# Smaller array tiles for the level and state matmuls of a gated linear attention, with a new order of issue

## The chip, the cores and the metric

The kernel runs on one core of one Trainium2 chip. The metric is the time on the device in microseconds (us), from the first to the last instruction; smaller is better. A profile is one execution taken by the hardware profiler.

## The reference

Two blocks follow each other. The first is a gated linear attention with complex decays: for every batch (4) and head (8), a 48 by 48 complex state is multiplied by a decay per row at each of 768 tokens, takes in the outer product of key and value, and is read by the query. The second is an MLP with a PReLU over all 3072 tokens.

```python
def _attn_ref(q, k, v, a_re, a_im):
    B, H, S, D = q.shape                      # 4, 8, 768, 48
    mag = np.sqrt(a_re * a_re + a_im * a_im)
    scale = np.minimum(mag, 0.999) / (mag + 1e-06)
    a_re_n, a_im_n = (a_re * scale, a_im * scale)
    ...
    for t in range(S):
        ar, ai = (a_re_n[:, :, t, :, None], a_im_n[:, :, t, :, None])
        new_re = ar * S_re - ai * S_im
        new_im = ar * S_im + ai * S_re
        kv = np.einsum('bhd,bhe->bhde', k[:, :, t], v[:, :, t])
        S_re, S_im = (new_re + kv, new_im)
        y[:, :, t] = np.einsum('bhd,bhde->bhe', q[:, :, t], S_re)
    return y

def _moe_ref(x, w_in, w_out, alpha):          # x: 3072 x 384, w_in: 384 x 2048, w_out: 2048 x 384
    h = x @ w_in
    g = np.maximum(h, 0.0) + alpha * np.minimum(h, 0.0)
    return (g @ w_out).astype(np.float32)
```

All matmuls are in fp32.

## The kernel before

The sequence is cut into chunks of 128 tokens; a **unit** is one chunk of one batch with all eight heads, so there are 24 units. The running products of the decays' phases and magnitudes come first (`gates`: VectorE, ScalarE, GpSimd; the results go through DRAM). In a unit, queries and keys are turned by the phases, so that real and imaginary parts stand as 96 rows (48 + 48). Inside a chunk, a pair of tokens (key s before query t) meets at exactly one **level** h of 1, 2, 4, 8, 16, 32: there the keys are those of the first half of a block of 2h tokens, the queries those of its second half. Each level thus has 64 keys and 64 queries for each head, and a mask keeps blocks of h by h on the diagonal. Between levels VectorE multiplies keys and queries by the decays over h tokens (`step`).

```python
    LEVELS = [1 << i for i in range(6)]
    ...
        def meet(name, weights, moving, n, *after):
            e = yield PE(0.467 * n / HC, ..., mode=1, n=8)
            t = ps.tile([P, HP, n], F32, tag="lv", name="ps_lv", bufs=2)     # HC = n = 64
            for p in range(4):
                for i in range(2):
                    nc.tensor.matmul(t[64 * i:64 * i + 64, p], lhsT=weights(4 * i + p),
                                     rhs=moving(KQ[:, 0, 4 * i + p]), start=True, stop=True)
        ...
        def mask_out(name, t, n, e):         # A[name] = ps_lv times the mask
            ...
            if name in by_row:               # h = 16 and 32: ScalarE, a mask by row
                for m, s in enumerate(by_row[name]):
                    cols = slice(m * name, (m + 1) * name)
                    nc.scalar.activation(a[:, :, cols], t[:, :, cols], AF.Copy, scale=s)
            else:                            # h = 1, 2, 4, 8: VectorE
                nc.vector.tensor_tensor(out=a, in0=t, in1=masks[name]..., op=ALU.mult)
```

A unit goes through six levels in turn: ScalarE copies the level's keys together (`W`, not for h = 1), TensorE lets them meet the queries (`ps_lv`), VectorE does the step, and the mask gives `A`.

```python
        for h in LEVELS:
            ...
                nc.scalar.copy(W..., halves(KQ[:, 1]..., h)[:, :, 0])
            e, t = yield from meet(h, weights, second(h), HC, w, k_)
            ...
            step(h)
            yield from mask_out(h, t, HC, e)
```

The two halves of a chunk then each give a **state product** (keys transposed, times values), one in the last chunk of a batch:

```python
        for n in range(H):                                          # 8 heads
            for s in range(1 if last else 2):                       # halves of 64 tokens
                rows = slice(HC * s, HC * (s + 1))
                nc.tensor.matmul(kv[s][:, n], lhsT=KT[rows, n],     # 64 rows, 96 weight columns
                                 rhs=V[rows, n // 2, (n % 2) * D:(n % 2 + 1) * D],
                                 start=True, stop=True)
```

The output `ps_y` sums the readout of the state (96 rows, 48 weight columns, 64 moving) and, for each level, values times `A` (64 by 48 weights, four tiles of the array). The MLP follows in groups of one or two chunks: `ps_h` (`w_in`), PReLU over ScalarE and VectorE (`g_sb`), `ps_o` (`w_out`).

The order in which all engines get their instructions is fixed while the program is built. A planner holds a model of engine times and, for each task (a gate group, a unit, the MLP, the loads), **due times** out of a table; at each point it issues, of the steps that can start within a small window, the one that is due first. A step on TensorE that would change the array's tiling is put back by `KEEP`.

```python
    KEEP = 569.0
    WINDOW = 0.185
    ...
            for task in self.tasks:
                t = self._start(task[1])
                ...
                    ready.append((first, not task[1][5], task[2][0] + self.KEEP * turn, len(ready), t, task))
            now = min(ready)[0] + self.WINDOW
            *_, t, task = min((r for r in ready if r[0] <= now), key=lambda r: r[1:4])
```

Of the kernel before, what the change touches and what calls it, by code (L numbers as in the profile page):

```python
# [9 lines left out]
F32 = mybir.dt.float32  # L10
U32 = mybir.dt.uint32
U16 = mybir.dt.uint16
AF = mybir.ActivationFunctionType
ALU = mybir.AluOpType
# [3 lines left out]
P = 128  # L18
# [26 lines left out]
class Plan:  # L45
# [6 lines left out]
    POOL = 0.4  # L52
# [3 lines left out]
    RATE = 215.0  # L56
    SWITCH = 0.095
    ENTER = (0.105, 0.048, 0.04, 0.053)
    KEEP = 569.0
    WINDOW = 0.185  # L60
    FETCH = 6.0
    COUNT = 84.0
    WAITS = 1.0107
# [71 lines left out]
                self.tasks.remove(task)  # L135


DUES = {'gates0': (-11979.6, -10892.9),
 'gates1': (174.7, -496.9),
 'gates2': (561.6, -311.9),  # L140
 'gates3': (3235.0, -200.5),
 'gates4': (1592.2, -63.0),
 'gates5': (4379.1, 219.4),
 'gates6': (489.8, 859.5),
 'gates7': (3140.3, 976.6),
 'gates8': (2306.3, 2393.8),
 'loads': (-377.6, 1731.8),
 'halves': (1898.2, -2044.1),
 'v': (-322.2, 1835.9),
 'raw': (2301.7, -5010.3),  # L150
 'in': (-1647.0, -796.9),
 'out': (3534.9, -230.2),
 'unit0': (-3641.5, -1502.8),
 'unit1': (-5353.3, -123.3),
 'unit2': (-1532.8, 1640.0),
 'unit3': (-36.9, 1543.1),
 'unit4': (-67.5, -25.0),
 'unit5': (-141.1, -113.0),
 'unit6': (1465.8, 2568.1),
 'unit7': (107.5, 119.9),  # L160
 'unit8': (181.8, 180.8),
 'unit9': (137.3, 195.5),
 'unit10': (387.8, 400.1),
 'unit11': (311.3, 312.9),
 'unit12': (681.4, 692.8),
 'unit13': (575.5, 570.7),
 'unit14': (910.0, 926.1),
 'unit15': (803.1, 798.4),
 'unit16': (1248.6, 1307.1),
 'unit17': (859.2, 964.8),  # L170
 'unit18': (1896.0, 2100.5),
 'unit19': (738.1, 831.9),
 'unit20': (913.8, 963.5),
 'unit21': (2733.6, 4210.5),
 'unit22': (-2826.2, 536.2),
 'unit23': (-402.2, 5283.7),
 'mlp': (-1586.9, 86.2)}

UNIT_STEPS = [-1.986, -14.344, -6.726, -1.525, -2.462, -10.149, -2.522, -4.692, -4.149, -10.103, -10.542, -0.315, -7.97,
 -6.489, -0.934, -9.318, -9.689, -5.484, -17.877, -60.052, -33.755, -3.423, -13.049, -34.345, -29.097, -2.452,  # L180
 -0.718, -31.551, 3.33, 0.026, 3.304, 6.38, -3.93, -14.011, -21.191, -7.962, -28.438, -0.376, -6.583, -1.248,
 -21.404, -25.972, -17.097, -22.461, 20.771, 1.493, -15.349, 0.052, 4.97, -13.972, 11.878, -14.379, 32.13,
 -21.617, 23.086, 22.986, 21.226, -2.184]


@with_exitstack
def kernel(
# [32 lines left out]
    nc = tc.nc  # L220
    B, HP, _, D, S = q.shape
# [5 lines left out]
    D2 = 2 * D  # L227
    HC = P // 2
# [13 lines left out]
    ps = ctx.enter_context(tc.tile_pool(name="ps", bufs=1, space=PSUM))  # L242

    def halves(t, h):

        return t.rearrange("p (n s h) -> p n s h", s=2, h=h)
# [4 lines left out]
    masks, by_row = {}, {}  # L251
# [16 lines left out]
    for h in (16, 32):  # L268
        by_row[h] = []
        for m in range(HC // h):  # L270
            t = consts.tile([P, 1], F32, tag=f"rows{h}_{m}", name=f"rows{h}_{m}")
# [6 lines left out]
    done = plan.done  # L278
# [5 lines left out]
        return "ACT", 0.17 + n * 0.85e-3, after, takes, 0, first  # L284

    def POOL(n, *after):
        return "POOL", 0.4 + n * 2.0e-3, after, (), 0, False

    def PE(us, *after, takes=(), mode=0, n=1):
        return "PE", us * plan.pace, after, takes, 0, False, mode, 4 * n  # L290

    def DMA(kb, *after, takes=(), engine="SP"):
        return engine, 0.45, after, takes, kb, False

    R = {name: Ring(n) for name, n in dict(
        KQ=3, PP=1, T=2, V=1, W=2, KT=1, St=3, yT=1, xT=2, raw0=1, raw1=1, raw2=1, g0=0, g1=0, g2=0, ot=2, top=2,
        lv=2, misc=1, y=1, h=2, o=1).items()}
# [250 lines left out]
    start = consts.tile([D2, B, H], F32, tag="start")  # L548
# [68 lines left out]
    def weights(name):  # L617
        for f in range(NF // 2):
            dst = w_in_sb[:, f] if name == "in" else w_out_sb[:, 2 * f:2 * (f + 1)]
            done["w_" + name, 2 * f] = done["w_" + name, 2 * f + 1] = yield from piece(dst, name, f)  # L620
# [102 lines left out]
    state = {}  # L723
# [5 lines left out]
    def unit(u):  # L729
# [3 lines left out]
        KQ, PP = L["KQ"], L["PP"]  # L733
# [2 lines left out]
        R["PP"].put(r)  # L736
        A, made = {}, []

        def meet(name, weights, moving, n, *after):

            e = yield PE(0.467 * n / HC, *after, *[("met", name, u - 1)] * (u > 0), takes=(R["lv"], R[name]), mode=1, n=8)
            t = ps.tile([P, HP, n], F32, tag="lv", name="ps_lv", bufs=2)
            for p in range(4):
                for i in range(2):
                    nc.tensor.matmul(t[64 * i:64 * i + 64, p], lhsT=weights(4 * i + p),  # L745
                                     rhs=moving(KQ[:, 0, 4 * i + p]), start=True, stop=True)
            done["met", name, u] = e
            return e, t

        def mask_out(name, t, n, e):  # L750

            if name in by_row:
                e = yield ACT(HP * name + 100, e)
            else:
                e = yield DVE(HP * n, e)
            a = A[name] = work.tile([P, HP, n], F32, tag=f"A{name}", name=f"A{name}",
                                    bufs=2 if name <= 4 else 1)
            if name in by_row:
                for m, s in enumerate(by_row[name]):
                    if m:  # L760
                        e = yield ACT(HP * name + 100, e)
                    cols = slice(m * name, (m + 1) * name)
                    nc.scalar.activation(a[:, :, cols], t[:, :, cols], AF.Copy, scale=s)  # L763
            else:
                a, t = [z.rearrange("p n (s t) -> p (n s) t", t=HC) for z in (a, t)]
                nc.vector.tensor_tensor(out=a, in0=t, in1=masks[name].unsqueeze(1).to_broadcast(
                    [P, HP * n // HC, HC]), op=ALU.mult)
            R["lv"].put(e)
            made.append(e)

        def second(h):
            return lambda t: halves(t, h)[:, :, 1]

        def step(h):

# [9 lines left out]
        if c == 0:  # L785
            k_ = yield DMA(144, *[("state", u - 2)] * (u > 1), takes=(R["St"],))
# [3 lines left out]
            k_ = yield DVE(H * D, k_, ("start", 0))  # L790
            nc.vector.tensor_tensor(out=St, in0=St, in1=start[:, b].unsqueeze(2).to_broadcast([D2, H, D]), op=ALU.mult)
            state[b] = (St, k_)
        k_ = r
        for h in LEVELS:
            w = k_
            if h == 1:
                weights = lambda n: KQ[:, 1, n].rearrange("p (m s) -> p m s", s=2)[:, :, 0]
            else:
                w = yield ACT(H * HC, k_, takes=(R["W"],))
                W = work.tile([D2, H, HC], F32, tag="W", name="W", bufs=2)  # L800
                nc.scalar.copy(W.rearrange("p n t -> p (n t)").rearrange("p (m h) -> p m h", h=h),  # L801
                               halves(KQ[:, 1].rearrange("p n t -> p (n t)"), h)[:, :, 0])
                weights = lambda n: W[:, n]
            e, t = yield from meet(h, weights, second(h), HC, w, k_)
            if h > 1:
                R["W"].put(e)
            k_ = yield DVE(2 * H * HC, e, *[("decays", u)] * (h == 1))
            T = L["T"]
            step(h)
            yield from mask_out(h, t, HC, e)  # L810
        q_ = k_

        last = c + 1 == NCH
        for i in range(2):
            e = yield PE(0.333, k_, takes=(R["misc"],), n=4)
            t = ps.tile([P, HP, D2], F32, tag="misc", name="ps_kt")
            for p in range(4):
                nc.tensor.transpose(t[:, p], KQ[:, 1, 4 * i + p], ident[:D2, :D2])  # L818
            e = yield ACT(HP * D2, e, takes=() if i else (R["KT"],))
            if i == 0:  # L820
                KT = work.tile([P, H, D2], F32, tag="KT", name="KT", bufs=1)
            nc.scalar.copy(KT[:, 4 * i:4 * i + 4], t)
            R["misc"].put(e)
        e = yield PE(1.395, e, ("V", u), *[("state", u - 1)] * (u > 0), takes=(R["misc"],) if last else (R["misc"], R["lv"]), mode=3, n=8 if last else 16)
        V = L["V"]
        kv = [ps.tile([D2, H, D], F32, tag=tag, name="ps_kv", bufs=n) for tag, n in (("misc", 1), ("lv", 2))[:2 - last]]
        for n in range(H):
            for s in range(1 if last else 2):
                rows = slice(HC * s, HC * (s + 1))
                nc.tensor.matmul(kv[s][:, n], lhsT=KT[rows, n], rhs=V[rows, n // 2, (n % 2) * D:(n % 2 + 1) * D],  # L830
                                 start=True, stop=True)
        R["KT"].put(e)
        states = [state.pop(b)]
        for s in range(1 if last else 2):
# [14 lines left out]
        g, cg = group_of[u]  # L849
        for s in range(2):  # L850
            before, known = states[s]
            e = yield PE(0.444, q_, known, takes=() if s else (R["y"],), mode=1, n=8)
            if s == 0:
                Y = ps.tile([P, 2, 512], F32, tag="y", name="ps_y")[:, :, 0:2 * P].rearrange(
                    "p i (s t) -> p i s t", s=2)
            for n in range(H):
                nc.tensor.matmul(Y[64 * (n % 2):64 * (n % 2) + D, n // 4, n // 2 % 2, HC * s:HC * (s + 1)],  # L857
                                 lhsT=before[:, n], rhs=KQ[:, 0, n, HC * s:HC * (s + 1)],
                                 start=(s == 0 and n // 2 % 2 == 0), stop=False)
            R["St"].put(e)  # L860
# [168 lines left out]
```

## Time and profile before

| what | value |
|---|---|
| time, median of three (lowest to highest) | 925.12 us (920.33 to 927.54) |
| TensorE busy, matmuls / weight loads | 756.7 us (82%) / 569.1 us (62%) |
| VectorE busy | 664.6 us (72%) |
| ScalarE busy | 412.2 us (45%) |
| GpSimd busy | 198.4 us (21%) |
| TensorE matmuls and weight loads recorded | 8384 each |
| DMA | 130.51 MB, 141 GB/s |

In the profile's lines, PE is TensorE's matmuls, PEld its weight loads, DVE VectorE, ACT ScalarE and POOL GpSimd. `L745` is line 745 of the kernel: L745 the levels, L830 the state products, L857 the state readout, L870 values times `A`, L917 `ps_h`, L936 `ps_o`, L783 the steps, L801 the copies `W`, L766 and L763 the masks. `96*64 96x64` after a matmul is its weights (rows by columns) and its moving operand (rows by columns). An fp32 matmul call shows as two records. The end of a matmul is modelled, so that busy times overlap; starts are measured. `issue` is time in which an engine waited for nothing that the profile shows; `q8 instruction` is the DMA queue that brings TensorE's instructions.

### The profile page before, as it was taken

The numbers are of one execution on the slowest core, as the hardware profiler recorded it, in microseconds if no ns is written. First come the engines' busy times: TensorE is split into PE (matmuls) and PEld (weight loads), VectorE is DVE, ScalarE is ACT, GpSimd is POOL, SyncE is SP. The second block draws the span as 40 slices with busy tenths as digits, with TensorE's granted clock in tenths as the row PEclk, the third lists the DMA queues.
The fourth block names the chain that finished last, engine by engine and source line by source line (L and its number), as shares of the span: only waits on it lengthen the run. The fifth ranks groups of instructions, "written<-read, shape, count | busy, mean of one in ns | idle before, by whom it ended". The sixth has DMA issues, their size and how long they took to land.

```text
span 923.7 us, 20680 instructions
## 1 busy us (share of the span) xinstructions
PE 756.7 (82%) x8384; PEld 569.1 (62%) x8384; DVE 664.6 (72%) x956; ACT 412.2 (45%) x897; POOL 198.4 (21%) x347
## 2 busy tenths in 40 slices
PE   0013423497998899999988999999999999999998
PEld 0002422375776677767766777777777777777776
DVE  5897988898997789979876977978674555531112
ACT  6554455364554456454754236543433333432111
POOL 4054183005400630280063015000700000000000
PEclk9999999999999999999998999999999999999999
DMA  8691985968778576958775586857565656420000
GB/s 223 147 270 52 222 217 163 242 155 166 141 191 193 120 161 150 208 101 190 194 142 108 164 185 124 181 117 169 115 138 109 131 121 112 104 61 18 18 9 18
DMA packets 194533, 130.51 MB, mean 141 GB/s; under 512 B 74504, under 2 KB 186248, under 8 KB 194440
## 3 DMA queue, kind: packets, MB, share of 16 engines
q1 hardware_dynamic: 194440, 129.20, 61.5%
q8 instruction: 66, 1.08, 0.5%
q14 instruction: 27, 0.22, 0.1%
HBM read 100.82 MB, written 35.71 MB: 148 GB/s over the span
## 4 chain that ended last, share of the span: by engine, by line
PE 67%; DVE 13%; POOL 9%; ACT 4%; issue 4%; DMA 1%; SPq 1%; DVEq 0%; ACTq 0%; POOLq 0%
PE ps_o L936 26%; PE ps_h L917 24%; PE ps_lv L745 7%; POOL gate L428 4%; POOL gate L430 4%; PE ps_y L870 3%; PE ps_kv L830 3%; PE ps_y L857 2%; DVE gate L428 2%; DVE KQ L783 2%; DVE gate L430 1%; PE ps_kt L818 1%; DVE gate L514 1%; POOL run L430 1%; DVE top L599 1%
## 5 line engine op out<-in xcount | busy, mean ns | idle before, releaser
L936 PE MATMUL ps_o<-w_out_sb,g_sb 128*128 128x384 f32 x768 | 301.7, 509 | 28.2 <-DVE g_sb L926 28.1
L917 PE MATMUL ps_h<-xT,w_in_sb 128*128 128x256 f32 (+1 forms) x1344 | 296.8, 356 | 3.3 <-issue 3.2
L917 PEld LDWEIGHTS ps_h<-xT,w_in_sb 128*128 128x128 f32 x1344 | 236.4, 193 | 76.5 <-issue 6.5
L926 DVE SCALAR_TENSOR_TENSOR g_sb<-g_sb,al,ps_h 128x256 f32<-128x256 f32 (+1 forms) x224 | 98.2, 439 | 170.4 <-ACT g_sb L924 169.1
L783 DVE TENSOR_TENSOR KQ<-KQ,T 96x1024 f32<-96x1024 f32 x144 | 176.2, 1234 | 32.8 <-PE ps_lv L745 29.4
L924 ACT ACTIVATE g_sb<-ps_h 128x256 f32<-128x256 f32 (+1 forms) x224 | 78.9, 353 | 257.7 <-PE ps_h L917 251.8
L936 PEld LDWEIGHTS ps_o<-w_out_sb,g_sb 128*128 128x128 f32 x768 | 132.9, 192 | 82.1 <-DVE g_sb L926 29.5
L745 PE MATMUL ps_lv<-KQ,W 96*64 96x64 f32 x1920 | 85.6, 239 | 70.5 <-ACT W L801 67.5
L745 PEld LDWEIGHTS ps_lv<-KQ,W 96*64 96x64 f32 x1920 | 70.7, 148 | 97.0 <-ACT W L801 76.3
L801 ACT COPY W<-KQ 96x512 f32<-96x512 f32 x120 | 74.6, 624 | 60.4 <-DVE KQ L783 59.0
L428 POOL TENSOR_TENSOR gate<-gate 128x72 f32<-128x72 f32 (+1 forms) x56 | 37.8, 674 | 146.9 <-ACT gate L458 143.2
L734 DVE TENSOR_TENSOR KQ<-KQ,PP 96x2048 f32<-96x2048 f32 x24 | 55.6, 2316 | 17.1 <-DMA PP<-phs 16.9
L745 PE MATMUL ps_lv<-KQ 96*64 96x64 f32 x384 | 17.8, 237 | 51.8 <-DVE KQ L734 50.0
L745 PEld LDWEIGHTS ps_lv<-KQ 96*64 96x64 f32 x384 | 14.8, 149 | 55.0 <-DVE KQ L734 50.2
L883 ACT COPY yT<-ps_y 48x256 f32<-48x256 f32 x96 | 30.9, 366 | 36.5 <-PE ps_y L870 33.9
L428 DVE TENSOR_TENSOR gate<-gate 128x576 f32<-128x576 f32 (+3 forms) x70 | 44.7, 639 | 1.7
L870 PE MATMUL ps_y<-A,VL 64*48 64x64 f32 x2304 | 42.7, 227 | 1.2 <-issue 1.2
L514 DVE TENSOR_TENSOR gate<-gate 128x1152 f32<-128x1152 f32 (+2 forms) x36 | 43.0, 1216 | 0.7 <-POOL gate L499 0.6
L830 PEld LDWEIGHTS ps_kv<-V,KT 64*96 64x96 f32 x704 | 37.0, 172 | 10.2 <-issue 6.8
L763 ACT ACTIVATE A<-ps_lv,rows 128x64 f32<-128x64 f32 x144 | 37.3, 331 | 12.6 <-PE ps_lv L745 12.2
L870 PEld LDWEIGHTS ps_y<-A,VL 64*48 64x48 f32 x2304 | 37.7, 126 | 8.0 <-issue 6.4
L430 POOL TENSOR_TENSOR gate<-gate 128x36 f32<-128x36 f32 (+1 forms) x56 | 40.5, 723 | 4.4
(94 smaller groups left out, 769.3 us busy)
## 6 DMA issues: line engine op xcount, KB each, us to landing
T<-decs SPq DMA_DIRECT2D x48, 384.0 KB
PP<-phs SPq DMA_DIRECT2D x48, 193.5 KB
KQ<-in_q_dram SPq DMA_DIRECT2D x48, 192.0 KB
decs<-gate SPq DMA_DIRECT2D x7, 1152.0 KB
phs<-gate SPq DMA_DIRECT2D x14, 576.0 KB
KQ<-in_k_dram SPq DMA_DIRECT2D x40, 192.0 KB
vsc<-in_v_dram SPq DMA_DIRECT2D x48, 144.0 KB
VL<-vsc SPq DMA_DIRECT2D x24, 288.0 KB
```

Source lines behind the costliest of these rows:

```text
L428: on(4 * k).tensor_tensor(out=m, in0=w[:, 1::-1].unsqueeze(2).to_broadcast([P, 2, 2, k]), in1=pairs_of(u), op=ALU.mult)
L430: on(2 * k).tensor_tensor(out=dst, in0=m[:, 0], in1=m[:, 1], op=ALU.add)
L734: nc.vector.tensor_tensor(out=KQ, in0=KQ, in1=bass.AP(tensor=PP.tensor, offset=PP.offset, ap=[PP.ap[0], (1, 2), (P + 1, H), (1, P)]), op=A ...
L745: nc.tensor.matmul(t[64 * i:64 * i + 64, p], lhsT=weights(4 * i + p), rhs=moving(KQ[:, 0, 4 * i + p]), start=True, stop=True)
L783: nc.vector.tensor_tensor(out=x, in0=x, in1=m, op=ALU.mult)
L801: nc.scalar.copy(W.rearrange("p n t -> p (n t)").rearrange("p (m h) -> p m h", h=h), halves(KQ[:, 1].rearrange("p n t -> p (n t)"), h)[:, ...
L830: nc.tensor.matmul(kv[s][:, n], lhsT=KT[rows, n], rhs=V[rows, n // 2, (n % 2) * D:(n % 2 + 1) * D], start=True, stop=True)
L870: nc.tensor.matmul(o, lhsT=Vp[h][64 * i:64 * i + 64, s, e_ * D:(e_ + 1) * D], rhs=a, start=False, stop=(h == LEVELS[-1] and s == 1))
L917: nc.tensor.matmul(p, lhsT=w_in_sb[:, f // 2, kk, f % 2 * P:(f % 2 + 1) * P], rhs=x_of[m][:, kk], start=(kk == 0), stop=(kk == NK - 1))
L924: nc.scalar.activation(gt, p, AF.Relu, scale=-1.0)
L926: nc.vector.scalar_tensor_tensor(out=gt, in0=gt, scalar=al_1[:, f:f + 1], in1=p, op0=ALU.mult, op1=ALU.add)
L936: nc.tensor.matmul(sums[0], lhsT=gt[:, c * P:(c + 1) * P], rhs=w_out_sb[:, f], start=(f == 0), stop=(f == NF - 1))
```

## The change

The matmuls of a level are cut to the blocks on the diagonal that the mask can keep: with h of at most 32, the first 32 keys only meet the first 32 queries, the second 32 the second. A level becomes 16 calls of 32 weight columns by 32 moving columns in place of 8 of 64 by 64, and writes four groups of 32 partitions, four column tiles of the array. `ps_lv` is half as wide; the mask's instructions read it twice. The state products are cut into three pieces of 32 weight columns: 48 calls in place of 16, on three column tiles by two row tiles. Both are meant to use more of the array at once. The planner's model is fitted anew (levels 0.28 in place of 0.467, state products 0.75 in place of 1.395), and with it the due times of all tasks, `KEEP` and `WINDOW`.

```diff
-    KEEP = 569.0
-    WINDOW = 0.185
+    KEEP = 180.0
+    WINDOW = 0.077
...
-DUES = {'gates0': (-11979.6, -10892.9),
- 'gates1': (174.7, -496.9),
...
- 'mlp': (-1586.9, 86.2)}
+DUES = {'gates0': (-5527.1, -5917.4),
+ 'gates1': (-86.9, -80.3),
...
+ 'mlp': (-3039.5, 582.0)}
...  (UNIT_STEPS, 58 numbers, replaced as well)
     def POOL(n, *after):
-        return "POOL", 0.4 + n * 2.0e-3, after, (), 0, False
+        return "POOL", 0.5 + n * 2.0e-3, after, (), 0, False
...
-            e = yield PE(0.467 * n / HC, ..., mode=1, n=8)
-            t = ps.tile([P, HP, n], F32, tag="lv", name="ps_lv", bufs=2)
+            e = yield PE(0.28, ..., mode=1, n=16)
+            t = ps.tile([P, HP, HC // 2], F32, tag="lv", name="ps_lv", bufs=2)
             for p in range(4):
                 for i in range(2):
-                    nc.tensor.matmul(t[64 * i:64 * i + 64, p], lhsT=weights(4 * i + p),
-                                     rhs=moving(KQ[:, 0, 4 * i + p]), start=True, stop=True)
+                    q_ = halves(KQ[:, 0, 4 * i + p], h)[:, :, 1]
+                    for g in range(2):
+                        j, m = HC // 2 * g, HC // (2 * h)
+                        nc.tensor.matmul(t[64 * i + j:64 * i + j + HC // 2, p], lhsT=weights(4 * i + p)[:, j:j + HC // 2],
+                                         rhs=q_[:, m * g:m * (g + 1)], start=True, stop=True)
...
-                    nc.scalar.activation(a[:, :, cols], t[:, :, cols], AF.Copy, scale=s)
+                    at = m * name % (HC // 2)
+                    nc.scalar.activation(a[:, :, cols], t[:, :, at:at + name], AF.Copy, scale=s)
             else:
-                a, t = [z.rearrange("p n (s t) -> p (n s) t", t=HC) for z in (a, t)]
-                nc.vector.tensor_tensor(out=a, in0=t, in1=masks[name].unsqueeze(1).to_broadcast(
-                    [P, HP * n // HC, HC]), op=ALU.mult)
+                whole = [P, HP, 2, HC // 2]
+                nc.vector.tensor_tensor(out=a.rearrange("p n (g t) -> p n g t", g=2), in0=t.unsqueeze(2).to_broadcast(whole),
+                                        in1=masks[name].rearrange("p (g t) -> p g t", g=2).unsqueeze(1).to_broadcast(whole),
+                                        op=ALU.mult)
...
-        e = yield PE(1.395, e, ("V", u), ..., mode=3, n=8 if last else 16)
+        e = yield PE(0.75, e, ("V", u), ..., mode=3, n=24 if last else 48)
...
-            for s in range(1 if last else 2):
-                rows = slice(HC * s, HC * (s + 1))
-                nc.tensor.matmul(kv[s][:, n], lhsT=KT[rows, n], rhs=V[rows, n // 2, (n % 2) * D:(n % 2 + 1) * D],
-                                 start=True, stop=True)
+            for j in range(0, D2, HC // 2):
+                for s in range(1 if last else 2):
+                    rows = slice(HC * s, HC * (s + 1))
+                    nc.tensor.matmul(kv[s][j:j + HC // 2, n], lhsT=KT[rows, n, j:j + HC // 2],
+                                     rhs=V[rows, n // 2, (n % 2) * D:(n % 2 + 1) * D], start=True, stop=True)
...
-            e = yield PE(0.444, q_, known, ..., mode=1, n=8)
+            e = yield PE(0.47, q_, known, ..., mode=1, n=8)
```

## The prediction

> **What bounds the kernel now.** I read the page's forty slices first, then the windows view (busy time by stage), then TensorE's waits, and last the timeline.
>
> ```profile
> PE   0013423497998899999988999999999999999998
> DVE  5897988898997789979876977978674555531112
> q8 instruction: 66, 1.08, 0.5%
> ```
>
> A slice is 23.1 us. TensorE has little to do in the first eight slices (185 us), while VectorE is busy; from there on it is full to the end. The windows view gives the same with numbers (columns: window, length, then busy us and instructions of PE, PEld, DVE, ACT, POOL, clock, DMA):
>
> ```profile
> 0.00:185.00 185.00, 45.55 (x652) 38.15 (x652) 153.03 (x243) 96.74 (x158) 63.01 (x106) 1.00 0.76 192
> 185.00:300.00 115.00, 104.22 (x1355) 81.57 (x1354) 100.63 (x149) 61.40 (x141) 24.29 (x44) 0.96 0.76 170
> 300.00:500.00 200.00, 188.00 (x2078) 138.66 (x2077) 166.84 (x214) 104.96 (x223) 74.16 (x116) 0.97 0.72 158
> 500.00:700.00 200.00, 198.83 (x2176) 147.46 (x2176) 157.41 (x209) 85.51 (x205) 36.88 (x80) 1.00 0.65 144
> ```
>
> So there are two stages. The head, 0 to 185 us, is bound by the gates' chain over VectorE, ScalarE and GpSimd; TensorE is idle for 139 of its 185 us. In the rest, 739 us, TensorE sets the end. Its waits, over the whole span, say the same (us in total, times, longest):
>
> ```profile
> PE ps_lv L745 <- ACT W L801: 67.5, 20, 15.5
> PE ps_lv L745 <- DVE KQ L734: 50.0, 2, 47.9
> PE ps_o L936 <- DVE g_sb L926: 28.1, 3, 25.0
> PE ps_lv L745 <- issue: 4.4, 3, 1.8
> PE ps_h L917 <- issue: 3.2, 1, 3.2
> ```
>
> The same view cut to the head holds 56.0, 50.0 and 25.0 us of the first three. After 500 us TensorE waits once in all, 1.2 us. **A microsecond of TensorE's time saved after 185 us is therefore worth about a microsecond at the end; one saved before it is worth next to nothing.**
>
> What a level and a state product occupy is read from starts, not from the modelled busy time. Timeline of TensorE (start, us, instructions merged):
>
> ```profile
> 501.92 1.46 PE L917 MATMUL ps_h<-xT,w_in_sb 128*128 128x256 f32 x6
> 503.31 1.15 PE L745 MATMUL ps_lv<-KQ,W 96*64 96x64 f32 x32
> 504.39 1.56 PE L936 MATMUL ps_o<-w_out_sb,g_sb 128*128 128x384 f32 x4
> ...
> 511.77 1.56 PE L830 MATMUL ps_kv<-V,KT 64*96 64x48 f32 x32
> 513.26 1.56 PE L917 MATMUL ps_h<-xT,w_in_sb 128*128 128x256 f32 x6
> ...
> 529.49 0.69 PE L745 MATMUL ps_lv<-KQ,W 96*64 96x64 f32 x16
> 530.11 1.56 PE L936 MATMUL ps_o<-w_out_sb,g_sb 128*128 128x384 f32 x4
> ```
>
> An fp32 call is two records, so one level (8 calls) is x16. From a start to the next line's start, two levels take 1.08 us and one 0.62: a level costs **0.46 us**, and leaving this tiling costs 0.62 - 0.46 = 0.16. Entering costs about 0.10 more (six ps_h records take 1.39 us ahead of ps_lv, 1.29 ahead of a full-array line at 505.79 to 507.08). A state product, x32, takes 1.49 - 0.15 for leaving = **1.34 us**, a little more in blocks entered from cold.
>
> **What the Trainium skill says.** "TensorEngine Tiling (Array Packing)", Key Properties: tiles run weight loads and matmuls in parallel, and a change of tiling drains the engine. The trace agrees on both: single records of ps_lv start in pairs, 7 ns apart in the pair and 58 ns from pair to pair (two column tiles side by side), and entering plus leaving costs the 0.26 us above. The same page, Instruction Overhead: about 60 cycles a matmul, and no tiling factor should be taken from a dimension that is already small. That would speak against 32 columns; but the ps_y line (64x64 tiles, four at once) starts records 7 ns apart, so the overhead isn't serial across tiles here. "TensorE: Matmul & The Clock Gate", LDWEIGHTS: a load's time goes with its columns. It fits the state product: two row tiles with 96 weight columns take 85 ns a pair for only 48 moving columns, whereas ps_y with 48 weight columns moves 64 columns on four tiles in 56 ns. The same page, Part 3, gives 2.38 times for three column tiles and 10.6 for sixteen tiles; no run here has shown 32-column tiles yet.
>
> **The change part by part.**
>
> *Levels.* A level's 64 keys by 64 queries need only the two diagonal 32x32 blocks (the mask drops the rest for block sizes to 32), so 8 calls become 16 with half the weight columns and half the moving columns, on four column tiles. Now: 8 rounds of two tiles at 58 ns = 0.46 us. After: 32 records in 8 rounds of four. A round is bound by its moving columns, half of 58 = 29 ns, or by starts, 4 x 7 = 28 ns. That makes 8 x 29 = 0.23 us; the diff's own planner figure is 0.28. I take 0.26 between them, so 0.20 saved. The windows view cut to L745 counts 992 + 1040 = 2032 records after 185 us, which is 127 of the 144 levels: 127 x 0.20 = **25.4 us**. The 17 levels of the head shorten a chain that waits for other engines: under 3 us, left out.
>
> *State products.* 16 calls become 48 with 32 weight columns, on three column groups by two row groups. Now 1.34. After: 96 records in 16 rounds of six; starts 6 x 7 = 42 ns, moving columns 48/64 x 56 = 42 ns: 0.67 us; the planner's figure is 0.75. I take 0.71, so 0.63 saved. Cut to L830 the windows view has 288 + 352 = 640 records after 185 us: 18 blocks of 32 and the four shorter ones of a batch's last chunk (16). 18 x 0.63 + 4 x 0.31 = **12.6 us**.
>
> *Mask-out.* VectorE still writes 128x256 elements (413 ns now, L766), reading the smaller ps_lv twice by a broadcast; ScalarE's instructions are the same in number and size. Nothing. The state readout (L857) is untouched; the planner's 0.47 in place of 0.444 is 1 us over all units, left out.
>
> *More instructions.* TensorE's 8384 + 8384 records grow by 144 x 32 for levels and 1408 x 2 for states, to 24,192. The instruction queue brings them in 66 packets of 1.08 MB, some 256 instructions each, so 29 more packets are needed, bunched in the new blocks. Issue waits of TensorE after 185 us are 3.2 + 1.8 + 1.2 = 6.2 us now. With 44% more instructions and denser bunches I take **5 us lost**.
>
> *Due times.* They alter nothing but order. From 185 us on the trace shows 169 visits to a tiling (94 levels, 22 states, 23 readouts, 30 outputs), at 0.26 us each 44 us in all: not less than what the change saves. The planner's penalty for a switch falls from 569 to 180 and its look-ahead from 0.185 to 0.077, which lets it switch more readily; I take 12 visits more, **3 us lost**, by choice rather than by reading.
>
> Sum: 25.4 + 12.6 - 5 - 3 = 30 us. 925 - 30 = **895 us**.
>
> **Rivals.** (1) *The 32-column tiles don't run four at once*: loads or starts become serial, a level stays near 0.42 us and a state near 1.1. Then 127 x 0.04 + 20 x 0.24 = 10 us are saved and 8 given back: about 923. Against it stands ps_y, whose four tiles hold 14 ns a record. (2) *VectorE becomes the bound.* From 185 to 700 us it is busy for 100.6 + 166.8 + 157.4 = 425 of 515 us, 82%; with 25 us of that stage gone it is 87%. A third of the gain could turn into waits of levels for VectorE, about 905; against it, MLP matmuls stand ready to fill, and 84 us of them are left over at the end. (3) *The new order is the larger part.* If the head gets filled with more TensorE work or switches become fewer, 875 to 880; if the new times stretch the head (139 us idle there, a 47.9 us first wait) or let fetches and switches bunch, 925 to 945.
>
> **Range and chances.** The tile arithmetic alone gives 38 saved, give or take 8; fetch and switches 8 lost, give or take 6; order in the head give or take 12. Together some 16 either way, more for rival 1: 873 to 918. The 2% line is at 906.6. Faster by over 2%: 0.75; within 2%: 0.17; slower by over 2%: 0.08.
>
> **What would show it.** Right: ps_lv reads 96*32 with x32 a level, 0.23 to 0.28 us from first start to last; ps_kv shows 64*32 with x96 in 0.67 to 0.75 us; the head is still about 185 us; TensorE stays at nine tenths from there to the end; q8 has about 95 packets. Wrong: a level stays over 0.4 us (rival 1); after 300 us ps_lv waits for W or KQ by tens of us (rival 2); issue waits over 15 us (fetch mis-sized); visits off by over 30, or the first full slice of TensorE a slice or more from where it is now (rival 3).

## The result and the profile after

The changed kernel takes 897.69 us (median of four, 891.59 to 900.16) against 922.73 us for the kernel before beside it: a ratio of 0.9716, 95% interval 0.9643 to 0.979. The prediction said 895. The sum came out; the two terms that make it up did not, and most of this part is about that.

The slices of the page, with the granted clock of TensorE and the queue that brings its instructions:

```profile
PE   0000143877979899999989999998999999999998
DVE  5997989998969898879878988895677555532112
PEclk9999995788989999999999999999999999999999
q8 instruction: 95, 1.56, 0.8%
```

95 packets are what the prediction worked out. TensorE stands at eight tenths in slice 8 already, where it stood at four before, so the head ends about a slice earlier. New are dips (7, 8) in TensorE's row after the head and half or reduced clock in slices 7 to 10 and 12. The windows view, columns as before:

```profile
0.00:185.00 185.00, 44.84 (x1140) 36.28 (x1140) 161.62 (x256) 103.09 (x175) 59.05 (x106) 0.92 0.80 200
185.00:300.00 115.00, 99.42 (x1925) 74.32 (x1926) 99.77 (x145) 57.77 (x128) 32.62 (x55) 0.90 0.70 163
300.00:500.00 200.00, 190.44 (x3365) 136.53 (x3365) 170.93 (x221) 108.45 (x236) 62.09 (x106) 0.98 0.73 163
500.00:700.00 200.00, 195.09 (x3268) 140.18 (x3268) 154.81 (x208) 88.62 (x210) 42.73 (x80) 0.98 0.70 153
```

Between 185 and 300 us TensorE is busy for less (99.4 in place of 104.2 us) and the clock is 0.90 in place of 0.96; from 500 to 700 us, where it was full, 195.1 in place of 198.8. So some of the time that the smaller tiles free is idle. TensorE's waits after the head (185 us on; us in total, times, longest):

```profile
PE ps_lv L748 <- issue: 7.0, 3, 3.3
PE ps_kt L822 <- ACT KT L826: 6.2, 2, 3.9
PE ps_h L922 <- DMA xT<-ysc: 4.0, 2, 2.5
PE ps_lv L748 <- ACT W L805: 4.0, 4, 2.7
PE ps_y L875 <- issue: 2.3, 2, 2.0
PE ps_o L941 <- issue: 1.8, 2, 1.6
```

Issue waits are 13.9 us in all (two kinds of 1.5 and 1.3 us are not shown), against 6.2 before. The blocks themselves, in the timeline:

```profile
500.46 0.46 PE L748 MATMUL ps_lv<-KQ,W 96*32 96x32 f32 x32
500.85 1.56 PE L941 MATMUL ps_o<-w_out_sb,g_sb 128*128 128x384 f32 x4
...
521.93 1.09 PE L835 MATMUL ps_kv<-V,KT 64*32 64x48 f32 x96
522.95 1.56 PE L941 MATMUL ps_o<-w_out_sb,g_sb 128*128 128x384 f32 x4
```

A level, with leaving, takes 0.39 us; leaving has become shorter (0.125 us by single records), so the level is 0.27. A state product takes 1.02 with leaving, so 0.89: less than the 1.34 of before, more than the 0.71 that I took.

### The profile page after: what moved, and what is told of

It reads as the page before. It is cut to its first block, busy times and chain, and to the rows that moved or that the text cites. A ratio compares the mean times of both kernels' runs of the same rounds, so it can differ in the third digit from the quotient of the medians.

```text
span 897.6 us, 28109 instructions
## 1 busy us (share of the span) xinstructions
PE 721.5 (80%) x12096; PEld 526.4 (59%) x12096; DVE 662.6 (74%) x956; ACT 412.8 (46%) x897; POOL 196.6 (22%) x347
## 4 chain that ended last, share of the span: by engine, by line
PE 52%; DVE 15%; DMA 10%; POOL 7%; SPq 7%; ACT 5%; issue 4%; DVEq 0%; ACTq 0%; POOLq 0%
PE ps_o L941 21%; PE ps_h L922 19%; SPq L714 4%; POOL gate L428 4%; PE ps_y L875 3%; PE ps_lv L748 3%; DMA PP<-phs 3%; DMA T<-decs 2%; POOL gate L430 2%; DVE gate L428 2%; PE ps_y L862 2%; PE ps_kv L835 2%; DVE KQ L787 2%; DVE gate L430 2%; DVE KQ L734 1%
## 5 line engine op out<-in xcount | busy, mean ns | idle before, releaser
L922 PE MATMUL ps_h<-xT,w_in_sb 128*128 128x256 f32 (+1 forms) x1344 | 300.8, 358 | 4.2 <-DMA xT<-ysc 4.0
L748 PE MATMUL ps_lv<-KQ,W 96*32 96x32 f32 x3840 | 56.3, 204 | 82.0 <-ACT W L805 70.9
L748 PEld LDWEIGHTS ps_lv<-KQ,W 96*32 96x32 f32 x3840 | 44.5, 116 | 110.7 <-ACT W L805 83.4
L428 POOL TENSOR_TENSOR gate<-gate 128x72 f32<-128x72 f32 (+1 forms) x56 | 40.6, 725 | 172.5 <-ACT gate L458 168.8
L748 PE MATMUL ps_lv<-KQ 96*32 96x32 f32 x768 | 12.0, 204 | 58.5 <-DVE KQ L734 57.1
L875 PE MATMUL ps_y<-A,VL 64*48 64x64 f32 x2304 | 44.7, 227 | 2.3 <-issue 2.3
L748 PEld LDWEIGHTS ps_lv<-KQ 96*32 96x32 f32 x768 | 9.5, 117 | 62.3 <-DVE KQ L734 57.3
L772 DVE TENSOR_TENSOR A<-ps_lv,mask 128x256 f32<-128x256 f32 x96 | 39.3, 413 | 0.0
```

What stands on the lines that cost most here:

```text
L428: on(4 * k).tensor_tensor(out=m, in0=w[:, 1::-1].unsqueeze(2).to_broadcast([P, 2, 2, k]), in1=pairs_of(u), op=ALU.mult)
L748: nc.tensor.matmul(t[64 * i + j:64 * i + j + HC // 2, p], lhsT=weights(4 * i + p)[:, j:j + HC // 2], rhs=q_[:, m * g:m * (g + 1)], start=T ...
L875: nc.tensor.matmul(o, lhsT=Vp[h][64 * i:64 * i + 64, s, e_ * D:(e_ + 1) * D], rhs=a, start=False, stop=(h == LEVELS[-1] and s == 1))
L922: nc.tensor.matmul(p, lhsT=w_in_sb[:, f // 2, kk, f % 2 * P:(f % 2 + 1) * P], rhs=x_of[m][:, kk], start=(kk == 0), stop=(kk == NK - 1))
```

## Experiments

In what follows, `work`, `waits` and `half clock` are worked out from the starts of all matmul records after 185 us. Each gap between two starts is compared with the mean gap of the same pair of shapes at full clock; an excess over 0.4 us counts as a wait, a smaller excess inside a stretch of half clock as half clock (time lost, not the length of the stretch), the rest is work. The three, and some 4 us at the very end, make up the span after the head.

### Tiles and order apart

Four kernels. Two keep one order and change the tiles: the planner's figures and due times stay, and with them the order of all instructions on all engines. Old tiles in the new order:

```diff
 # the changed kernel's planner figures and due times
-  16 calls of 32 x 32 for a level, 48 of 32 weight columns for a state product
+   8 calls of 64 x 64,             16 of 96 weight columns
```

> The changed kernel's order (its planner figures and due times), but with the levels at 64 by 64 and the state products at 96 weight columns as before. Theory 1 (the tiles bring the gain, the order brings little): TensorE's work after the head grows by the 25 us of the levels and 11 us of the state products that the changed kernel's blocks save, so 926 to 938 us, and issue waits and instruction packets fall back to about 6 us and 66. Theory 2 (the new order brings most of it): under 912 us.

Measured: 906.36 us, ratio 0.9835 (0.9801 to 0.9868). New tiles in the old order (the reverse edit in the kernel before):

> The order of the kernel before, with the new tiles for levels and state products. Theory 1: 923 less 36 for the shorter blocks, plus about 6 for more instruction packets, so 885 to 900 us, as fast as the changed kernel or a little faster. Theory 2: over 910 us, as the order was made for longer blocks and TensorE then waits for W and KQ.

Measured: 918.44 us, ratio 0.9957 (0.9934 to 0.9979). Then each part of the tiles alone, in the new order:

> The changed kernel with its state products put back to 16 calls of 96 weight columns; order kept. Theory 1: 11 us slower than the changed kernel less some 2 us for 11 packets fewer, so 904 to 912 us. Theory 2: within 4 us of the changed kernel.

Measured: 892.49 us, ratio 0.9685 (0.965 to 0.9719).

> The changed kernel with its levels put back to 64 by 64; order kept. Theory 1: 25 us slower than the changed kernel less some 4 us for 18 packets fewer, so 914 to 926 us. Theory 2: within 8 us of the changed kernel.

Measured: 903.25 us, ratio 0.981 (0.9768 to 0.9851).

**Theory 1 falls in all four.** Theory 2 holds in three; of the levels alone it had said within 4 us of the changed kernel, and they are 5 us under it. The order alone is worth some 16 us. The tiles are worth 4 us in the old order and about 9 in the new (5 by the later run of the changed kernel, below). The levels alone in the new order do at least as well as both parts together. The table has the accounts of the profiled executions (us; "last ps_y" is the start of the last attention matmul, "tail" what follows it, MLP matmuls alone). The profiled execution of the states only is 6 us faster than their median; a second profile of the changed kernel gives 662, 37 and 12 us of work, waits and half clock.

| kernel | span | work | waits | half clock | last ps_y | tail | packets |
|---|---|---|---|---|---|---|---|
| before | 924 | 700 | 26 | 8 | 832 | 92 | 66 |
| old order, new tiles | 921 | 669 | 50 | 13 | 829 | 92 | 95 |
| new order, old tiles | 904 | 697 | 16 | 2 | 829 | 75 | 66 |
| new order, states only | 895 | 687 | 18 | 2 | 820 | 75 | 77 |
| new order, levels only | 891 | 672 | 26 | 5 | 816 | 75 | 84 |
| changed kernel | 898 | 661 | 34 | 13 | 822 | 75 | 95 |

Two things stand in it. First, the work does shrink as predicted: 31 us in the old order, 36 in the new. Of that, waits and half clock take back 29 in each (24 + 5, and 18 + 11). Second, the order works through the tail. The kernel before, and the new tiles in the old order, have 92 us of MLP left when attention ends; everything in the new order has 75, because more MLP is placed in the gaps of attention. A part of it lies in the head: there the old tiles in the new order keep TensorE busy for 54.69 us, where the prediction's windows have 45.55, and do 85 MLP records in place of 44.

```profile
0.00:185.00 185.00, 54.69 (x717) 46.11 (x718) 160.28 (x256) 101.87 (x173) 58.87 (x106) 1.00 0.81 201
```

Timeline at the end of attention, of the kernel before:

```profile
830.57 1.59 PE L870 MATMUL ps_y<-A,VL 64*48 64x64 f32 x96
832.09 1.13 PE L917 MATMUL ps_h<-xT,w_in_sb 128*128 128x256 f32 x4
```

and of the old tiles in the new order:

```profile
827.43 1.61 PE L869 MATMUL ps_y<-A,VL 64*48 64x64 f32 x96
828.96 1.56 PE L935 MATMUL ps_o<-w_out_sb,g_sb 128*128 128x384 f32 x4
```

The end of attention hardly differs; the span does, by 20 us. In the account these are 3 us of work, 10 of waits and 6 of half clock. Nothing in the tail uses the new tiles, so no tile can shorten it. Where the shorter blocks went in the old order is in the waits after 185 us of the new tiles there:

```profile
PE ps_lv L748 <- ACT W L806: 18.1, 16, 3.4
PE ps_lv L748 <- issue: 11.9, 7, 4.4
PE ps_y L863 <- DVE St L847: 8.9, 7, 2.5
```

They were 11.5, 1.8 and 1.9 us in the kernel before. TensorE comes sooner to a point in its fixed order where the next operand, or the next instruction, isn't there.

Where along the span this happens shows when one and the same matmul is followed through two kernels of one order. In the old order the new tiles are level with the old ones as late as 518 us (0.2 us earlier), in the new order as late as 577 us (0.2 us earlier). Up to there the shorter blocks bring nothing. By the end of attention they are 2.6 and 6.5 us earlier. The chain of work that ended last has a likely reason: long after the head it still runs through the gates on GpSimd. Its last longer gate pieces (start, us, what), with the old tiles in the old order and in the new:

```profile
478.21 2.67 POOL gate L430
544.43 2.50 POOL gate L428
```

In the kernel before, GpSimd has 22% of this chain from 300 to 490 us, and from 600 to 800 us all of it is TensorE's. With the new tiles in the old order TensorE loses its share to loads (DMA) and to the instructions that issue them (SPq). The whole chain before, and with the new tiles in the old order:

```profile
PE 67%; DVE 13%; POOL 9%; ACT 4%; issue 4%; DMA 1%; SPq 1%; DVEq 0%; ACTq 0%; POOLq 0%
PE 40%; DVE 16%; POOL 13%; DMA 10%; SPq 10%; issue 6%; ACT 4%; DVEq 0%; ACTq 0%; POOLq 0%
```

From 600 to 800 us the load of a unit's phases, which has a single buffer (`PP`), takes 15.5% of it, and the issue of loads of values (L714) 12.5%. The chain is inferred from semaphores, and no run here changes the gates or the loads. That they hold the shorter blocks back is not shown.

### Instructions or data?

That leaves two theories for the 29 us. F: the supply of instructions. The new blocks use up 256 instructions faster than the next packet comes, TensorE runs dry, and the clock then falls to half for 3.4 us. W: a faster TensorE runs into other engines' data. I first counted waits over 0.75 us whose end follows the landing of an instruction packet by 1.2 to 1.7 us. With a packet every 8 us, some 6% of unrelated waits would fall there by chance.

| kernel | such waits | us, whole gaps | other waits, us |
|---|---|---|---|
| before | 4 of 11 | 10.0 | 14.4 |
| old order, new tiles | 10 of 28 | 18.3 | 31.5 |
| new order, old tiles | 2 of 8 | 2.3 | 13.2 |
| new order, states only | 6 of 13 | 6.0 | 13.7 |
| new order, levels only | 4 of 13 | 4.9 | 20.5 |
| changed kernel | 9 of 17 | 18.5 | 15.3 |

In the new order the packets' share grows with the two parts together far more than with each alone (2.3, 4.9, 6.0, 18.5). To test it, levels with half the instructions and nearly the same length:

```diff
-            for p in range(4):              # 16 calls, 32 weight columns by 32 moving
+            for p in (0, 2):                # 8 calls, 32 weight columns by 64 moving: two heads' queries
```

> The changed kernel with levels of 8 calls in place of 16, each with 32 weight columns and 64 moving columns (two heads' queries meet one head's keys, so half of the keys are left out): about the same length of a level, 0.23 to 0.27 us, with half its instructions, 77 packets in place of 95. Theory F: waits after the head fall from 34 to about 20 us and half-clock time with them, 882 to 891 us. Theory W: the waits stay, 895 to 899 us.

Measured: 886.2 us, ratio 0.9594 (0.9551 to 0.9637), 12 to 15 us under the changed kernel. A level became 0.22 us, not 0.27, and work fell by 3 us in the sum. Packets are 77, waits at packets 5.2 us in place of 18.5, half clock 7 in place of 13. But the sum of waits fell only from 34 to 31, because other waits rose:

```profile
PE ps_lv L748 <- ACT W L805: 9.0, 8, 5.1
PE ps_kt L822 <- ACT KT L826: 8.1, 3, 4.1
PE ps_h L922 <- DMA xT<-ysc: 2.8, 3, 1.8
```

So F holds in part, and its price is the half clock as well as the wait; some 3 us are the shorter levels, and W stands right behind it. The second test was meant to hold the instructions' number apart from the state products' length:

```diff
-            for j in range(0, D2, HC // 2):            # three pieces of 32 weight columns
+            for j0, j1 in ((0, 64), (64, 96)):         # 64 and 32 weight columns
```

> The changed kernel with its state products in pieces of 64 and 32 weight columns, on two by two tiles: 32 calls in place of 48, a block about as long (16 rounds at 56 to 58 ns, 0.90 to 0.93 us), some 5 instruction packets fewer. Theory F (the gain is lost to the supply of instructions: the new blocks use up 256 instructions faster than the next packet comes, TensorE runs dry and its clock then falls to half for 3.4 us): 890 to 896 us, with fewer waits that end just after a packet. Theory W (a faster TensorE runs ahead into waits for other engines' data, whatever the number of instructions): 897 to 900 us.

Measured: 949.88 us, ratio 1.0305 (1.0265 to 1.0345). It tells neither theory apart, as the block isn't of the same length:

```profile
507.70 3.73 PE L835 MATMUL ps_kv<-V,KT 64*64 64x48 f32 x64
```

3.5 us from first start to last: single records show 130 to 150 ns at each change between 64 and 32 columns, fifteen times a block. It tells something else: 57 us more of work (22 blocks by 2.6) cost 52 us of time. Work added to TensorE is paid nearly in full, work taken away is not.

Then W by itself: two of the six steps of VectorE left out (48 instructions of 1.235 us, 59 us), once with each tile set.

```diff
-            step(h)
+            if h > 2:
+                step(h)
```

> The changed kernel without VectorE's steps for h = 1 and 2, which leaves out 48 instructions of 1.235 us, 59 us of VectorE's work; order kept. Theory W (with the short blocks TensorE is held by its data, which comes round over ScalarE and VectorE in the fixed order): the waits of TensorE after the head shrink and the last ps_y comes earlier, 865 to 880 us. Theory F (the supply of instructions alone holds it): within 8 us of the changed kernel, as the packets stay 95.

Measured: 885.37 us, ratio 0.9594 (0.9554 to 0.9633).

> The same two steps left out with the old tiles in the new order. Theory W: here TensorE's own work fills the stretch, so that less is won than with the new tiles, 893 to 902 us against 906; what the two tile sets differ by grows from 8 us to 20 or more. Theory F: the difference stays at 8 to 10 us.

Measured: 898.09 us, ratio 0.9723 (0.9685 to 0.9761). The 59 us less on VectorE bring 12 to 16 us with the new tiles and 8 with the old. The tiles are then worth 13 us, more than 9, less than the 20 that W asked for; with them TensorE's waits after the head hardly change (32 us, from 34), and half clock falls from 13 to 4. Neither theory alone holds. VectorE's speed isn't what the rest of the waits hang on; which handoff of the ring does it (queries and keys on VectorE, copies on ScalarE, matmuls), or whether the gates and loads of the chain do, is not settled.

### What bounds a block

```diff
-  moving columns: 32 in a level, 48 in a state product
+  moving columns: 16,            24   (the rest is left out)
```

> The changed kernel with half the moving columns in levels (16 in place of 32) and state products (24 in place of 48); the mask and the state take the half that is there twice, so half of these products is left out. It measures what sets a block's length. If starts bound it (some 8 to 9 ns a record): a level stays 0.26 to 0.27 us and a state product 0.88 to 0.90. If moving columns bound it: 0.14 and 0.45. If the weight loads of 32 columns do: about 0.23 and 0.46.

Measured: 891.13 us, in a single execution. A level and a state product in the timeline:

```profile
510.99 0.45 PE L748 MATMUL ps_lv<-KQ,W 96*32 96x16 f32 x32
...
517.46 1.01 PE L838 MATMUL ps_kv<-V,KT 64*32 64x24 f32 x96
```

From first start to last a level stays 0.263 us, as it should if starts bind it, and a state product goes from 0.889 to 0.825. But the starts of single records (medians over all blocks at full clock) say otherwise. A **round** is one record on each tile; after the first, which is longer, a round takes:

| tiles at once, weight columns each | moving columns | round, ns |
|---|---|---|
| four, 32 (level) | 32 | 32 |
| four, 32 (level) | 16 | 32 |
| three, 32 (state product, last chunk) | 24 | 32 |
| six, 32 (state product, first rounds) | 24 | 32 |
| three, 32 (state product, last chunk) | 48 | 42 |
| six, 32 (state product, first rounds) | 48 | 42 |
| six, 32 (state product, from about the 30th record) | 24 or 48 | 50 |

Six tiles can start a record every 5.3 ns (32 over 6), so starts at 8.2 ns don't bind a level. Nor do its moving columns. What the rounds of 32 ns share is the 32 weight columns. The kernel before fits: 58 ns with 64 weight columns (levels), 85 with 96 (state products). So a level's round goes with its weight columns, as one tile's weight load would. The state product has the 42 ns a round of the prediction's term in its first rounds only; from about the 30th record on a round takes 50 ns, whatever its moving columns, which is 8.3 ns a record. That is what the term missed. What sets this rate is not shown; two levels in a row (x64) also slow down, from 32 to 34 ns a round.

### The order by its own figures, and the best of both

Levels alone, with the planner given the right figures for the old state products, so that it finds another order with the same due times:

```diff
-        e = yield PE(0.75, e, ..., mode=3, n=24 if last else 48)
+        e = yield PE(1.395, e, ..., mode=3, n=8 if last else 16)
```

> The levels in 32 by 32 tiles, the state products as before with the planner's figures of before for them (1.395 and 16 calls), all else as in the changed kernel, so that the order differs a little. If the order made for the right lengths helps, 884 to 891 us, better than with the wrong figures (892.5); if small changes of order without new due times only shift waits, 890 to 905 us.

Measured: 940.8 us, ratio 1.0211 (1.0166 to 1.0257). Work is as with the wrong figures (674 us against 672), but waits are 65 us in place of 26, half clock 16 in place of 5, and the tail grew from 75 to 124 us. The due times belong to the exact figures they were found with: two constants moved, and 48 us are lost.

Last, levels in small tiles with small state tiles only where one row tile works alone (the four last chunks):

```diff
+            if last:      # three pieces of 32 weight columns
+                ...
+                continue
             for s in range(2):      # 96 weight columns, as before
```

> Levels in 32 by 32 tiles; state products in 32 columns only in the four last chunks, where one row tile works alone (0.69 us in place of 1.39), and as before in the other twenty; order kept. If the bunched instructions of the state products cost more than their 0.45 us a block bring: 887 to 892 us, 4 to 9 us under the changed kernel run beside it. If the difference of the earlier runs was scatter: equal to it within 3 us.

Measured: 893.29 us, ratio 0.9685 (0.9653 to 0.9716).

> The changed kernel as it is, on the same chip as its neighbours: 895 to 900 us under either theory.

Measured: 901.39 us, ratio 0.9766 (0.9729 to 0.9802). The two intervals don't meet: leaving the small tiles out of twenty state products is worth 8 us, though TensorE's work is 9 us more (670 against 661). With the levels alone, at the same ratio, it is the fastest of the kernels that leave nothing out. The page's clock and packets, to be set against the changed kernel's:

```profile
PEclk9999995797999999999999999999999999999999
q8 instruction: 85, 1.39, 0.7%
```

Waits at packets are 4.3 us in place of 18.5, half clock 4 in place of 13.

## Why the prediction was right in the sum and wrong in its steps

*"A microsecond of TensorE's time saved after 185 us is therefore worth about a microsecond at the end."* This step failed. TensorE was full in the slices, and work added to it is paid nearly in full (52 us of time for 57). But 36 us taken away brought some 9, and 31 in the old order brought 4. A full row of slices shows that TensorE had no slack, not that the others had any. Every engine's order is fixed, so a shorter block can end in a wait for the next operand. The cut into two stages at 185 us was wrong as well: in the kernel before, the gates are on the chain that ended last until some 480 us, and 992 of the 2032 level records that the prediction counted lie before 500 us.

*Due times: "They alter nothing but order", 3 us lost.* This failed the other way: the order alone is worth 16 us. I read it in the number of visits (181 in place of 169, as assumed) and not where it acts, in how much MLP is left when attention ends, 92 us before and 75 after. They stood in the timeline of before (832 to 924 us); rival 2 counts 84 us of them as left over, and I drew nothing from it. Rival 3 named the order as the larger part, by a head filled with more TensorE work, and was right in that, though not in its 875 to 880 us.

*Levels, 25.4 us.* Right in size: 0.27 us for 0.26 taken, and 25 us less work with the levels alone. A round goes with the weight columns, though, not with moving columns or starts. *State products, 12.6 us.* Mis-sized: 0.89 in place of 0.71, as the rounds of 42 ns grow to 50 after some 30 records; the four last chunks, read as half a block, had been as long as a whole one (x16 in 1.31 us from first start to last), and are 0.68 now. Work fell by 10 us with the states only. In time they bring nothing that is clear of scatter by themselves (903.25 against 906.36), and beside the levels they cost 8 us.

*What set the old state product's length.* I put its 85 ns a pair down to the loads of 96 weight columns, with the Trainium skill's "TensorE: Matmul & The Clock Gate", LDWEIGHTS: a load's time goes with its columns. The rounds of 32, 58 and 85 ns for 32, 64 and 96 weight columns agree, and so does the lone row tile of a last chunk, which took 85 ns a record as well, as if each tile had its own loads. The kernel with pieces of 64 and 32 has pairs with 64 columns 93 ns apart, but it changes tiles at every other pair.

*More instructions, 5 us lost.* The 95 packets are exact; the loss is larger. Issue waits after the head rise by 7.7 us (6.2 to 13.9). By the count above, in the new order waits at packets go from 2.3 to 18.5 us and half clock from 2 to 13, though not all of the half clock follows such a wait. The prediction named the bunches and set their price too low: what counts is how many instructions stand close together.

*Rivals.* Rival 1 fell: four tiles run at once (a round of four in 32 ns). Rival 2 named VectorE; data waits are there, but 59 us less on VectorE don't end them.

So 33 for the tiles less 3 for the order, 30, was predicted, and 9 + 16 = 25 measured: tiles overvalued by 24 us and an order undervalued by 19 nearly cancelled each other. That the number was met says nothing for the steps.

## What to carry to other kernels

Before counting a faster engine's savings one for one, ask which other engine has to be earlier too; with fixed orders on all engines, test it with the old order and the new block. Read the chain of work that ended last by stretch before you say which engine bounds a stage. Judge a change of order by the work that is left for the end. Where many small matmuls replace few, count instructions per microsecond in the densest stretch: a wait for instructions costs itself and the half clock behind it.

## What the runs showed of the hardware

A round of fp32 records, one on each tile, took 32, 58 and 85 ns with 32, 64 and 96 weight columns a tile, where the moving columns were as many or fewer. That held for three, four and six tiles side by side with 32 weight columns, and for one and two row tiles with 96. With 32 weight columns and 48 or 64 moving ones it took 42 and 56 ns. In long blocks of small tiles a record started only every 8.3 to 8.5 ns from about the 30th on, where six tiles had begun with one every 5.3 to 7 ns. A change between 64 and 32 columns inside a block cost a gap of 130 to 150 ns where the tiles' own rounds had 60 to 86. After waits of some microseconds TensorE's clock stood at half for 3.4 us or a multiple: 37 us after the head in the changed kernel, 10 with the old tiles in the same order.
